# A set of seven half products in layer 1 of blocks 3 to 6, fixed staging tiles, C11 grown on M1, and a later check of the bounds

## The chip, the cores and the metric

The kernel runs on one core of a Trainium2 chip. The metric is the device time of one execution in microseconds (us). Times of engines come from one profiled execution.

## The reference, cut to what matters

B = 8 batches, H = 8 heads, S = 576 tokens, D = 64, 16 beacon keys ahead of the keys, DM = H * D = 512, rank 32, hidden width FF = 2048.

```
k_all  = concat(beacon_k, k);  v_all = concat(beacon_v, v)
scores = q @ k_all^T / sqrt(D);  masked causally over the S keys, beacons open
x      = softmax(scores) @ v_all            # per head, then heads side by side: (B, S, 512)
h      = (x^T @ U) @ V                      # mixes the 576 tokens of a batch, rank 32
u      = x + h^T
out    = u + max(u @ w_ch1, 0) @ w_ch2      # 512 -> 2048 -> 512
```

## The kernel before

**Tiling.** The attention goes by batch and pair of heads, the mixer by batch, and the two layers of the perceptron by blocks of 512 tokens, nine blocks (0 to 8) over all 8 x 576 tokens. All matrix work is in float16 with float32 sums. The transposed u (`uT`) lies in SBUF as a ring, channels on partitions; `uT` is made by transposing DMAs from x (`xb`) and by adding the mixer's products on VectorE (L476).

**One stream of work.** Every block of the perceptron is cut into small units of work, which go into one queue (`queue`). The attention code for the next batches calls `fill(n)` (L1180) between its own steps, and each call takes n units from the queue; so TensorE's instructions alternate between attention and perceptron. `fill` also issues one waiting step of the list `coming` (loads, weights made by GpSimd) per unit, and stores that have become due. Every engine runs its instructions in the order in which they were issued. `long_slot` (L1383) is the hand-written order for the later batches, `visit` (L395) does scores and exps in it, `mix` (L1250 and on) puts the mixer's steps into the queue, the loop at L1435 to L1466 goes over the pairs of heads.

**PSUM.** Eight banks go round in the order of their freeing: `pst` (L108) takes one, `emptying` (L115) gives it back.

**Layer 1.** Block 0 is computed plainly (`mlp_units`, L922). For blocks 1 to 8 `fast_units` (L595) makes the units. In blocks 1 to 6 layer 1 is sixteen `g_unit`s (L628 to L647): each is one tile of 128 hidden channels by 512 tokens, four matmuls (eight where the block wraps round the ring, as in block 4), whose relu is done by VectorE in units 2, 5, 11 and 13 and by ScalarE in the others. In blocks 7 and 8 (`QUADS`, L1163) layer 1 is done by `g_quads` (L649): three sets of four channel tiles each are computed as a 2 x 2 block product by seven half products in place of eight, in the manner of Strassen and Winograd. `step(q, n)` (L700 and on) is one step of set q: step 0 forms a product in bank A, which ScalarE copies to `lk`, and one in bank F, to which VectorE adds the copy; step 1 lets A grow by a second product (copied again) and begins D; step 2 lets A grow a third time (copied again), and VectorE adds the copy to D; step 3 ends A (relu by ScalarE) and D (sum and relu by VectorE). One half product is four matmuls of 256 columns (L674). The sums of weights that this needs (`lw`) are made by GpSimd (`quad_weights`, L580, four operations a set, L588), those of u by VectorE (L655, four a block), at the start of the block. A copy of bank A must be done before TensorE lets A grow again.

**Layer 2.** It is a 2 x 2 block product by seven products M1 to M7 in blocks 1 to 8; its sums of the hidden layer, called s1 to s4 in `sums` (L624), are made by VectorE while layer 1 still goes on (`SUMS`, L1164). In blocks 1 to 6 the units are `c_unit`s (L833), two a product, 14 in all; after each product `after(k)` (L795) adds: product 0 (bank A, M1) is copied by ScalarE, product 1 (bank F) is added to the copy by VectorE and gives C11, and C22, C21 and C12 follow. `residual` (GpSimd, L780) then adds u to each of the four quarters, from the tile `ut`, to which SP's queue transposes `uT` back (L611, issued in every second unit of layer 1); the quarter is then stored. In blocks 7 and 8 `chain_units` (L842) lets some products grow on one another's banks.

**Staging.** The q and k of a batch are loaded to two tiles of a pool `stage` with two buffers (`qk_tiles`, L253). Shortly before block 7, `quad_tiles` (L569) takes tiles from the same pool for the sums of weights, for those of u and for the copies of bank A.

**The check of the bounds.** `guard` (L997) is nine VectorE operations, which test the reciprocals of the softmax's sums; it is called once, right after the last mixer step has been put into the queue, and so falls into layer 1 of block 6. `guard_sum` (L1009) adds the result over partitions on TensorE; it stands in block 7. The answer decides at a branch near the end whether the slow exact path runs.

## Time and profile before

| | |
|---|---|
| time, median of 3 runs | 335.64 us (335.51 to 335.74) |
| the profiled execution | 336.39 us |
| its span | 334.5 us |
| TensorE busy | 326.3 us, 98% |
| VectorE, ScalarE, GpSimd busy | 251.7, 190.8, 148.5 us |
| layer 1 of blocks 3, 4, 5, 6, 7, 8 begins at | 146.00, 180.58, 215.32, 249.90, 279.1, 304.3 us |

The span is the time from the first to the last instruction in the profile; the execution's own time is 1.9 us longer. In the lines, PE is TensorE's matmuls, PEld its loads of weights, DVE VectorE, ACT ScalarE, POOL GpSimd, SP SyncE, which issues most DMAs (SPq is its queue). A line of the timeline gives the start, the time from there to the end of the last of the xN instructions, the engine, the line of the program, the operation, out<-in with shape and type, and in brackets how long the engine had been idle and what released it. A line of a group gives the busy time and the mean ns of one operation behind the bar.

### The profile page before, as it was taken

Reading aid. Unit: us, or ns where it says so; the run is one execution under the profiler, and the core shown is the slowest. Engines: PE = TensorE matmul, PEld = TensorE weight load, DVE = VectorE, ACT = ScalarE, POOL = GpSimd, SP = SyncE. Lnnn points to the kernel's source line nnn. Section 1 sums busy time; section 2 is a strip of 40 time slices with the busy share of each in tenths; the row PEclk is TensorE's granted clock in tenths of the full one; section 3 lists DMA queues with packets and bytes.
Section 4 is the critical chain, followed back from the end, with each engine's and each line's share of the span. In section 5 each row is a group of like instructions: output and inputs, shape, how many; then the busy total and the mean of one; then the engine's idle time right before and its main releaser. Section 6 shows DMA issues by size and latency. Waiting matters only on the chain.

```text
span 334.5 us, 9085 instructions
## 1 busy us (share of the span) xinstructions
PE 326.3 (98%) x3614; PEld 223.9 (67%) x3614; DVE 251.7 (75%) x572; ACT 190.8 (57%) x413; POOL 148.5 (44%) x185
## 2 busy tenths in 40 slices
PE   8899999999999999999999999999999999999993
PEld 3565555555577656865588888754875588788793
DVE  6675888678897668765777677667777978797692
ACT  5967961788972677257734684469435403703700
POOL 8987824766236540677066904150398014010010
PEclk9999999999999999999999999999999999999999
DMA  8999999999999993999999996955213513206113
GB/s 164 144 176 161 158 201 196 199 184 151 81 150 150 135 181 74 130 200 171 151 124 174 144 132 110 117 130 120 51 42 94 91 47 110 49 32 127 31 36 101
DMA packets 150561, 41.99 MB, mean 126 GB/s; under 512 B 131312, under 2 KB 149936, under 8 KB 150512
## 3 DMA queue, kind: packets, MB, share of 16 engines
q0 software_dynamic: 87568, 18.18, 73.3%
q1 hardware_dynamic: 62144, 22.41, 36.5%
q10 hardware_dynamic: 800, 0.75, 0.7%
q8 instruction: 30, 0.49, 0.6%
q14 instruction: 19, 0.16, 0.2%
HBM read 37.45 MB, written 9.44 MB: 140 GB/s over the span
## 4 chain that ended last, share of the span: by engine, by line
PE 91%; ACT 5%; DVE 1%; issue 0%
PE gps L635 24%; PE po L427 8%; PE mpsD L760 6%; PE sps L409 6%; PE mpsF L760 4%; PE cps L965 4%; PE mpsA L854 4%; PE gps L939 4%; PE mpsE L760 3%; PE qpsA L674 3%; PE mpsC L760 3%; PE mpsA L760 3%; PE mpsB L760 3%; ACT expt L376 2%; PE mpsD L854 2%; PE gps L663 2%
## 5 line engine op out<-in xcount | busy, mean ns | idle before, releaser
L418 ACT ACTIVATE expt<-sps 128x496 f16<-128x496 f32 (+2 forms) x192 | 82.2, 547 | 41.6 <-PE sps L409 41.6
L635 PE MATMUL gps<-uT,w 128*128 128x512 f16 (+1 forms) x448 | 91.9, 349 | 0.2 <-ACT kT L1091 0.2
L780 POOL TENSOR_TENSOR ob<-ob,ut 128x512 f32<-128x512 f32 x26 | 31.3, 1207 | 131.2 <-DVE ob L780 121.5
L760 PEld LDWEIGHTS <-gT 128*128 128x128 f16 x704 | 66.4, 98 | 10.4 <-issue 2.6
L635 PEld LDWEIGHTS <-w 128*128 128x128 f16 x448 | 40.4, 98 | 32.0 <-issue 2.5
L646 ACT ACTIVATE gT<-gps 128x512 f16<-128x512 f32 x72 | 42.9, 619 | 25.2 <-PE gps L635 19.9
L624 DVE TENSOR_TENSOR gT<-gT 128x1024 f16<-128x1024 f16 (+3 forms) x90 | 47.5, 550 | 1.0
L240 POOL DMA_DIRECT2D vs<-in_v_dram x50 | 39.9, 812 | 14.1 <-DMA w<-in_moe_w_ch_dram 11.1
L427 PEld LDWEIGHTS <-expt 128*128 128x128 f16 x900 | 33.8, 98 | 9.8 <-issue 1.5
L427 PE MATMUL po<-vs,expt 128*128 128x65 f16 x900 | 36.4, 194 | 0.3
L348 DVE TENSOR_TENSOR expt<-expt,bigmask 128x768 f16<-128x768 f16 x54 | 34.4, 676 | 1.4 <-ACT expt L418 1.2
L436 DVE TENSOR_TENSOR xb<-po,rec 128x320 f16<-128x320 f32 x64 | 31.5, 492 | 2.2
L435 DVE RECIPROCAL rec<-po 128x5 f32<-128x5 f32 x64 | 12.1, 189 | 19.5 <-PE po L427 19.1
L644 DVE TENSOR_SCALAR gT<-gps 128x512 f16<-128x512 f32 x24 | 16.6, 690 | 13.1 <-PE gps L635 12.6
L686 ACT ACTIVATE lk<-qpsA 128x512 f32<-128x512 f32 x18 | 10.3, 597 | 25.6 <-PE qpsA L674 14.8
L409 PE MATMUL sps<-qT,kT 64*128 64x80 f16 (+4 forms) x288 | 22.6, 281 | 0.0
L376 ACT ACTIVATE expt<-sps 128x496 f16<-128x496 f32 (+2 forms) x48 | 20.4, 569 | 0.7 <-PE sps L370 0.7
L854 PEld LDWEIGHTS <-gT 128*128 128x128 f16 x208 | 19.0, 98 | 2.4
L1038 POOL DMA_DIRECT2D st<-in_q_dram x20 | 16.9, 866 | 6.9 <-DVE ob L780 6.5
L409 PEld LDWEIGHTS <-kT 64*128 64x128 f16 x288 | 10.3, 94 | 12.8 <-issue 8.2
L1038 POOL DMA_DIRECT2D st<-in_k_dram x20 | 16.9, 859 | 1.5 <-DMA st<-in_q_dram 1.5
L939 PE MATMUL gps<-uT,w 128*128 128x512 f16 x64 | 16.2, 380 | 0.1
(151 smaller groups left out, 479.3 us busy)
## 6 DMA issues: line engine op xcount, KB each, us to landing
out_dram<-ob SPq DMA_DIRECT2D x33, 256.0 KB, 3.6
vs<-in_v_dram POOLq DMA_DIRECT2D x18, 128.0 KB, 6.9
w<-in_moe_w_ch_dram POOLq DMA_DIRECT2D x4, 512.0 KB, 6.4
w<-in_moe_w_ch_dram POOLq DMA_DIRECT2D x2, 1024.0 KB, 12.8
st<-in_k_dram POOLq DMA_DIRECT2D x12, 128.0 KB, 6.3
st<-in_q_dram POOLq DMA_DIRECT2D x12, 128.0 KB, 7.0
st<-in_k_dram POOLq DMA_DIRECT2D x4, 288.0 KB, 11.8
st<-in_q_dram POOLq DMA_DIRECT2D x4, 288.0 KB, 12.9
```

The lines of the kernel that those rows point to most:

```text
L240: nc.gpsimd.dma_start(out=dst[a : a + nq[j], j, :, :], in_=src[hs, ds(q0[j], nq[j]), :].rearrange("h p d -> p h d"))
L348: nc.vector.tensor_tensor(out=e, in0=e, in1=bigmask[:, :, :].rearrange("p (a b) x -> p a b x", b=2), op=ALU.min)
L409: nc.tensor.matmul(banks[i][:, ds(at0 + o, w)], kT(hp, c, ch), qT[hp, c, ds(qa, w)], start=True, stop=True, skip_group_check=len(unit) > 1,)
L418: nc.scalar.activation(out=at[p][3][i][:, ds(AT[g], gw[g])], in_=bank[:, ds(at0, gw[g])], func=AF.Exp, scale=scale)
L427: nc.tensor.matmul(po[:, j, :], ex[0 : nk[c], ds(blk[(c, j)], P)], vs[0 : nk[c], ds(c * H * E + h * E, E)], start=(c == 0), stop=(c == j),)
L436: nc.vector.tensor_tensor(out=xb[:, :, ds(h * D, D)], in0=po[:, :, 0:D], in1=r.broadcast_to([P, NT, D]), op=ALU.mult)
L624: nc.vector.tensor_tensor(out=o[:, ds(d0, n)], in0=x[:, ds(d0, n)], in1=y[:, ds(d0, n)], op=op)
L635: nc.tensor.matmul(g[:, ds(o, w)], w1[:, cc, ts(dc, P)], uT[:, cc, ds(at, w)], start=(cc == 0 and o == 0), stop=(cc == NCC - 1), skip_grou ...
L646: nc.scalar.activation(out=cell["g"][:, dc, :], in_=g, func=AF.Relu)
L760: nc.tensor.matmul(ps, a()[:, d, ds(P * i, P)], bm[:, d, ds(c0, w)], start=fresh and d == 0 and i == 0, stop=d == HF - 1, skip_group_check ...
L854: nc.tensor.matmul(ps, a()[:, d, ds(P * i, P)], bm[:, d, ds(c0, w)], start=fresh and d == 0, stop=d == HF - 1, skip_group_check=True,)
L1038: coming.append(lambda d=dst, s=src, a=m[j] - nq[j], n=m[j], j=j: nc.gpsimd.dma_start(out=d[a:n, j, :, :], in_=s[:, ds(q0[j], nq[j]), :].r ...
```

## The change

1. **One set in blocks 3 to 6.** `PARTS` takes the place of `QUADS`: blocks 3 to 6 do one set of four channel tiles (0, 1, 8, 9) by seven half products, the twelve other tiles as before; blocks 7 and 8 do three sets as before. The sixteen units are ordered tile 2, step 0, tile 10, step 1, tile 3, step 2, tile 11, tile 4, step 3, tiles 12, 5, 13, 6, 14, 7, 15. The plain tiles at places 2, 11 and 13 have their relu by VectorE. The sums s1 to s4 move to later units.
2. **Sums of u ahead.** For these four blocks the four subtractions of u are issued in the c-units 10 to 13 of the block before (`AHEAD`), by VectorE for blocks 3 and 4 and by GpSimd for blocks 5 and 6.
3. **C11 grown on M1.** In blocks 3 to 6 product 1 grows on product 0's banks, half by half; ScalarE copies the halves of M1 and later those of C11. Bank F and VectorE's add of C11 go.
4. **Fixed staging tiles.** Four constant tiles `staged` take the place of the pool `stage`; a batch uses the pair of its parity. The sums of u and of the weights of sets 1 and 2, and the copies of bank A for these sets, lie in parts of them; set 0's weights lie in tiles of the pool `pairs` and are made once, at an earlier pair of heads than before.
5. **The check later.** `guard` is put into the queue behind C11 of block 7, ahead of the unit whose result VectorE adds next; `guard_sum` stands three units later than before.

```diff
+    staged = [const.tile([P, TJ * DM], F16, name=f"st{i}", tag=f"st{i}") for i in range(4)]
-    def qk_tiles():
-        t = [stage.tile([P, TJ * DM], F16, name=f"st{i}", tag=f"st{i}") for i in range(2)]
+    def qk_tiles(b=0):
+        t = staged[2 * (b % 2) : 2 * (b % 2) + 2]
...
+    def quad_tiles(q):
+        if q == 0:
+            w = [pairs.tile([P, 512], F16, name=f"lw{k}", tag=f"pr{k % 2}") for k in range(4)]
+        else:
+            w = [staged[q - 1][:, ds(512 * k, 512)] for k in range(4)]
+            f = staged[q + 1][:, 0 : 2048].bitcast(F32).rearrange("p (k i x) -> p k i x", k=2, i=2)
+            lq["k", q] = (f[:, 0], f[:, 1], f[:, 0])
+        lq["w", q] = [x.rearrange("p (c f) -> p c f", c=2) for x in w]
+    def u_sums(t0, eng):
+        b11, b12, b21, b22 = (u_half(t0, c, x) for c in (0, 2) for x in (0, HT))
+        t1, t2, t3, t4 = (staged[i][:, 5 * DM : 6 * DM].rearrange("p (c x) -> p c x", c=2) for i in range(4))
+        lq["t"] = [t1, t2, t3, t4]
+        def one(o, x, y):
+            eng.tensor_tensor(out=o, in0=x, in1=y, op=ALU.subtract)
+        return [lambda a=a: one(*a) for a in ((t1, b12, b11), (t2, b22, t1), (t3, b22, b12), (t4, b21, t2))]
...
+            if not quads:
+                slots = [2, (0, 0), 10, (0, 1), 3, (0, 2), 11, 4, (0, 3), 12, 5, 13, 6, 14, 7, 15]
+                late = {11: ((0, 0, 4),), 12: ((1, 0, 4),), 13: ((2, 0, 4),), 14: ((0, 4, 3),), 15: ((1, 4, 3),)}
...
+        if parts:
+            sums_at = {0: ((2, 4, 3),), 1: ((0, 7, 1), (1, 7, 1)), 2: ((2, 7, 1), (3, 0, 4)), 3: ((3, 4, 4),)}
...
+        def second_on(i, c0, w):
+            ps = grown(1, "A", i, c0, w)
+            if i == 0:
+                out_tile("11")
+            nc.scalar.activation(out=obs["11"][:, i, :], in_=ps, func=AF.Copy)
+            freed(("A", i, c0))
+            if i:
+                residual("11", 0, 0)
         def c_unit(k, j):
-            bank = products[k][0]
-            p = pieces(bank)[j]
-            product(*products[k], *p)
+            p = pieces(products[k][0])[j]
+            if parts and k < 2:
+                (first, second_on)[k](*p)
+            else:
+                product(*products[k], *p)
...
+            for u in ahead(2 * k + j) if ahead else ():
+                u()
-            if j == 1:
+            if j == 1 and not (parts and k < 2):
                 after(k)
...
-    QUADS = (7, 8)
+    PARTS = {3: 1, 4: 1, 5: 1, 6: 1, 7: 3, 8: 3}
+    AHEAD = 10
...
+                us.extend(u_sums(512 * t, nc.vector if t < 5 else nc.gpsimd))
...
+            if p == P6 + 3:
+                quad_tiles(0)
+                coming.extend(quad_weights(0))
             if p == NP - 3:
-                quad_tiles()
-                coming.extend([u for q in range(3) for u in quad_weights(q)])
+                for n in (1, 2):
+                    quad_tiles(n)
+                    coming.extend(quad_weights(n))
...
         mix(B - 1)
-        guard()
-        queue.insert(len(queue) - 37, guard_sum)
+        queue.insert(len(queue) - 41, guard)
+        queue.insert(len(queue) - 34, guard_sum)
```

More of the change, by code (lines that the diff above doesn't have):

```diff
@@ L92 @@
     const = ctx.enter_context(tc.tile_pool(name="const", bufs=1))
-    stage = ctx.enter_context(tc.tile_pool(name="stage", bufs=2))
     pairs = ctx.enter_context(tc.tile_pool(name="pairs", bufs=2))
@@ L506, in end @@
             settle(1, uT[:, :, ds(u0 % RING + QM, n)], ups)
+            settled.add(u0 // S)
             emptying(ups)
@@ L565, in halves_of_w2, with u_half @@
         ]
-    lq = {}
-    def quad_tiles():
-        t = [stage.tile([P, TJ * DM], F16, name=f"lw{i}", tag=f"st{i}") for i in range(2)]
-        w = [[x[:, ds(512 * k, 512)] for k in range(4)] for x in t]
-        w.append([pairs.tile([P, 512], F16, name=f"lw{k}", tag=f"pr{k % 2}") for k in range(4)])
-        lq["w"] = [[x.rearrange("p (c f) -> p c f", c=2) for x in y] for y in w]
-        lq["t"] = [x[:, ds(4 * 512 + 512 * k, 512)].rearrange("p (c x) -> p c x", c=2) for x in t for k in range(2)]
-        f = [stage.tile([P, 3, 512], F32, name=f"lk{i}", tag=f"st{i}") for i in range(2)]
-        k = [x[:, i, :].rearrange("p (i x) -> p i x", i=2) for x in f for i in range(3)]
-        lq["k"] = [(k[2 * q], k[2 * q + 1], k[2 * q]) for q in range(3)]
+    lq, settled = {}, set()
+    def quad_tiles(q):
[6 more added lines that the diff above has]
+        lq["w", q] = [x.rearrange("p (c f) -> p c f", c=2) for x in w]
+    def u_half(t0, c0, x):
+        return uT[:, ds(c0, 2), ds((t0 + x) % RING, HT)]
+    def u_sums(t0, eng):
[3 more added lines that the diff above has]
+        def one(o, x, y):
+            assert (t0 + 511) // S in settled
+            eng.tensor_tensor(out=o, in0=x, in1=y, op=ALU.subtract)
+        return [lambda a=a: one(*a) for a in ((t1, b12, b11), (t2, b22, t1), (t3, b22, b12), (t4, b21, t2))]
     def quad_weights(q):
@@ L585, in quad_weights @@
         a11, a12, a21, a22 = part(0, 2 * q), part(2, 2 * q), part(0, HF + 2 * q), part(2, HF + 2 * q)
-        s1, s2, s3, s4 = lq["w"][q]
+        s1, s2, s3, s4 = lq["w", q]
         return [
@@ L593, in quad_weights, with fast_units @@
         ]
-    def fast_units(t0, dst, last=False, quads=False):
+    def fast_units(t0, dst, last=False, parts=0, ahead=None):
         cell, banks, obs = {}, {}, {}
+        quads = parts > 1
         cols = u_cols(t0, 512)
@@ L630, in g_unit, with between, layer_one @@
                 begin()
-            dc = order[k]
+            def between():
+                if k % 2 and cell["turns"]:
+                    cell["turns"].pop(0)()
+                for x in SUMS.get(k, ()):
+                    sums(*x)
+            layer_one(order[k], k in (2, 5, 11, 13), between)
+        def layer_one(dc, on_vector, between=lambda: None):
             g = pst([P, 512], F32, name="gps")
@@ L638, in g_unit @@
                     )
-            if k % 2 and cell["turns"]:
-                cell["turns"].pop(0)()
-            for x in SUMS.get(k, ()):
-                sums(*x)
-            if k in (2, 5, 11, 13):
+            between()
+            if on_vector:
                 nc.vector.tensor_scalar_max(out=cell["g"][:, dc, :], in0=g, scalar1=0.0)
@@ L649, in g_quads, with plain @@
         def g_quads():
-            at = t0 % RING
-            b11, b12, b21, b22 = (uT[:, ds(c, 2), ds(at + x, HT)] for c in (0, 2) for x in (0, HT))
+            b11, b12, b21, b22 = (u_half(t0, c, x) for c in (0, 2) for x in (0, HT))
+            us = u_sums(t0, nc.vector)
             t1, t2, t3, t4 = lq["t"]
-            us = [
-                lambda o=o, x=x, y=y: nc.vector.tensor_tensor(out=o, in0=x, in1=y, op=ALU.subtract)
-                for o, x, y in ((t1, b12, b11), (t2, b22, t1), (t3, b22, b12), (t4, b21, t2))
-            ]
             held = {}
-            def plain(dc):
-                g = pst([P, 512], F32, name="gps")
-                for cc in range(NCC):
-                    nc.tensor.matmul(
-                        g, w1[:, cc, ts(dc, P)], uT[:, cc, ds(at, 512)], start=cc == 0, stop=cc == NCC - 1
-                    )
-                nc.scalar.activation(out=cell["g"][:, dc, :], in_=g, func=AF.Relu)
-                emptying(g)
+            def plain(k, dc):
+                layer_one(dc, not quads and k in (2, 11, 13))
             def half(q, bank, a, b, fresh):
@@ L682, in of_lw, with space @@
             def of_lw(q, k):
-                return lambda c, i: lq["w"][q][k][:, c, ts(i, P)]
+                return lambda c, i: lq["w", q][k][:, c, ts(i, P)]
+            def space(q, k):
+                if k < 2:
+                    cell["k", q, k] = lq["k", q][k] if q else kept("k")
+                else:
+                    cell["k", q, k] = cell["k", q, 0]
+                return cell["k", q, k]
             def copied(q, k):
-                nc.scalar.activation(out=lq["k"][q][k], in_=held[q, "A"], func=AF.Copy)
+                nc.scalar.activation(out=space(q, k), in_=held[q, "A"], func=AF.Copy)
             def summed(q, bank, k, d, x):
                 nc.vector.tensor_tensor(
-                    out=cell["g"][:, ds(d, 2), ds(x, HT)], in0=held[q, bank], in1=lq["k"][q][k], op=ALU.add
+                    out=cell["g"][:, ds(d, 2), ds(x, HT)], in0=held[q, bank], in1=cell["k", q, k], op=ALU.add
                 )
@@ L720, in step, with unit @@
                     relu(cell["g"][:, :, HT:512].rearrange("p (h d) t -> p h d t", h=2)[:, :, ds(d, 2), :])
+            if not quads:
+                slots = [2, (0, 0), 10, (0, 1), 3, (0, 2), 11, 4, (0, 3), 12, 5, 13, 6, 14, 7, 15]
+                late = {11: ((0, 0, 4),), 12: ((1, 0, 4),), 13: ((2, 0, 4),), 14: ((0, 4, 3),), 15: ((1, 4, 3),)}
+                def unit(k, slot):
+                    if k == 0:
+                        begin()
+                    plain(k, slot) if isinstance(slot, int) else step(*slot)
+                    if k % 2 and cell["turns"]:
+                        cell["turns"].pop(0)()
+                    for x in late.get(k, ()):
+                        sums(*x)
+                return [lambda k=k, slot=slot: unit(k, slot) for k, slot in enumerate(slots)]
             slots = [
@@ L734, in unit @@
                 if isinstance(slot, int):
-                    plain(slot)
+                    plain(k, slot)
                 else:
@@ L831, in fast_units, with grown, first @@
         ]
-        def c_unit(k, j):
-            bank = products[k][0]
-            p = pieces(bank)[j]
-            product(*products[k], *p)
+        def grown(k, name, i, c0, w):
+            _, a, bm, _ = products[k]
+            fresh = (name, i, c0) not in banks
+            if fresh:
+                banks[name, i, c0] = pst([P, w], F32, name="mps" + name)
+            ps = banks[name, i, c0]
+            for d in range(HF):
+                nc.tensor.matmul(
+                    ps, a()[:, d, ds(P * i, P)], bm[:, d, ds(c0, w)],
+                    start=fresh and d == 0, stop=d == HF - 1, skip_group_check=True,
+                )
+            return ps
+        def first(i, c0, w):
+            ps = grown(0, "A", i, c0, w)
+            if i == 0:
+                kept("s1")
+            nc.scalar.activation(out=cell["s1"][:, i, :], in_=ps, func=AF.Copy)
+        def second_on(i, c0, w):
+            ps = grown(1, "A", i, c0, w)
+            if i == 0:
+                out_tile("11")
[3 more added lines that the diff above has]
+                residual("11", 0, 0)
+        def c_unit(k, j):
+            p = pieces(products[k][0])[j]
+            if parts and k < 2:
+                (first, second_on)[k](*p)
+            else:
+                product(*products[k], *p)
             for x in sums_at.get(2 * k + j, ()):
                 sums(*x)
-            if j == 1:
+            for u in ahead(2 * k + j) if ahead else ():
+                u()
+            if j == 1 and not (parts and k < 2):
                 after(k)
@@ L845, in chain_units @@
             small = [(0, 0, HC), (1, 0, P), (1, P, P)] if last else halves
-            def grown(k, name, i, c0, w):
-                _, a, bm, _ = products[k]
-                fresh = (name, i, c0) not in banks
-                if fresh:
-                    banks[name, i, c0] = pst([P, w], F32, name="mps" + name)
-                ps = banks[name, i, c0]
-                for d in range(HF):
-                    nc.tensor.matmul(
-                        ps, a()[:, d, ds(P * i, P)], bm[:, d, ds(c0, w)],
-                        start=fresh and d == 0, stop=d == HF - 1, skip_group_check=True,
-                    )
-                return ps
-            def first(i, c0, w):
-                ps = grown(0, "A", i, c0, w)
-                if i == 0:
-                    kept("s1")
-                nc.scalar.activation(out=cell["s1"][:, i, :], in_=ps, func=AF.Copy)
             def second(i, c0, w):
@@ L917, in fast_units @@
             return g_quads() + chain_units()
-        units = [lambda k=k: g_unit(k) for k in range(NDC)]
+        units = g_quads() if parts else [lambda k=k: g_unit(k) for k in range(NDC)]
         units += [lambda k=k, j=j: c_unit(k, j) for k in range(7) for j in range(len(pieces(products[k][0])))]
@@ L1023, in load_batch @@
         if b < DT0:
-            Ls[b] = qk_tiles()
+            Ls[b] = qk_tiles(b)
             emit_loads(b, Ls[b], vss[b % 2])
@@ L1030, in load_whole @@
     def load_whole(b):
-        Ls[b] = qk_tiles()
+        Ls[b] = qk_tiles(b)
         for i, (src, m) in enumerate(((k[b], nk), (q[b], nq))):
@@ L1191, in fill, with sums_ahead, at @@
             n -= 1
+    def sums_ahead(t):
+        if PARTS.get(t, 0) != 1:
+            return None
+        us = []
+        def at(n):
+            if n == AHEAD:
+                us.extend(u_sums(512 * t, nc.vector if t < 5 else nc.gpsimd))
+            return us[n - AHEAD : n - AHEAD + 1] if n >= AHEAD else []
+        return at
     def feed(b):
@@ L1203, in feed @@
             else:
-                units = fast_units(512 * t, dst, t == NBLK - 1, t in QUADS)
+                units = fast_units(512 * t, dst, t == NBLK - 1, PARTS.get(t, 0), sums_ahead(t + 1))
             queue.extend(units)
@@ L1272 @@
         emit_w1(0)
-        Ls[1] = qk_tiles()
+        Ls[1] = qk_tiles(1)
         (kt, qt), _ = Ls[1]
```

## The prediction

> **What bounds the kernel now.** I read the head of the profile's page first, then its chain of work that ended last, then busy time by stage (cut where TensorE starts a block's layer 1), then timelines of single engines around each edit.

> ```profile
> span 334.5 us, 9085 instructions
> ...
> PE 326.3 (98%) x3614; PEld 223.9 (67%) x3614; DVE 251.7 (75%) x572; ACT 190.8 (57%) x413; POOL 148.5 (44%) x185
> ...
> PE 91%; ACT 5%; DVE 1%; issue 0%
> ```

> TensorE is busy 98% of the span and is 91% of the chain that ended last. So a matmul saved shortens the kernel by its duration, and a pause of TensorE lengthens it by the pause.

> The stages (columns: stretch, its length, then busy time and instructions of PE, PEld, DVE, ACT, POOL; granted clock; DMA share; GB/s):

> ```profile
> 146.00:180.58 34.58, 34.58 (x374) 22.83 (x373) 24.78 (x52) 20.76 (x45) 18.44 (x22) 1.00 1.76 162
> 180.58:215.32 34.74, 34.74 (x437) 28.97 (x436) 24.77 (x52) 20.77 (x45) 16.42 (x20) 1.00 1.50 134
> 215.32:249.90 34.58, 34.58 (x373) 22.78 (x372) 24.99 (x51) 20.76 (x45) 14.82 (x13) 1.00 0.46 82
> 249.90:279.10 29.20, 29.20 (x270) 19.42 (x269) 23.43 (x47) 8.74 (x15) 11.16 (x10) 1.00 0.33 75
> ```

> These four rows are blocks 3 to 6, the ones whose layer 1 changes. TensorE pauses in none of them. VectorE, ScalarE and GpSimd have 6 to 20 us idle in each, so the sum of their added work fits; what matters is whether single results come in time.

> **The change part by part.**

> *1. Fewer products (blocks 3 to 6).* Rows of the chain, the last a run of 256-column matmuls:

> ```profile
> 146.00 0.86 PE gps L635 x4
> ...
> 150.03 4.42 PE gps L635 x20
> ...
> 219.35 4.42 PE gps L635 x20
> ...
> 284.63 1.31 PE qpsA L674 x12
> ```

> A 512-column matmul takes 0.865 / 4 = 0.216 us (a plain unit of four; 4.42 / 20 = 0.221 has what stands between units in it), one of 256 columns 1.31 / 12 = 0.109. Per block 16 x 0.216 = 3.46 become 28 x 0.109 = 3.06: -0.40, four times -1.6.

> *2. ScalarE's copies, blocks 3 and 4.* The growing bank A is copied by ScalarE after its first, second and third state, and TensorE's next matmuls into it wait for the copy. After unit 2 ScalarE has four exps to do, and by the order of instructions they stand ahead of the second copy. Block 3 now:

> ```profile
> 149.86 2.01 ACT L418 ACTIVATE expt<-sps 128x496 f16<-128x496 f32 x4 [1.05 <-PE sps L409]
> 151.73 1.12 ACT L646 ACTIVATE gT<-gps 128x512 f16<-128x512 f32 x2
> ...
> 279.75 0.60 ACT L686 ACTIVATE lk<-qpsA 128x512 f32<-128x512 f32 x1 [11.39 <-PE qpsA L674]
> ```

> and for the step from one engine to TensorE, block 7 (VectorE's sums, then the two TensorE products that need them):

> ```profile
> 279.99 0.41 DVE L655 TENSOR_TENSOR lw<-uT 128x512 f16<-128x512 f16 x1
> 280.44 1.26 DVE L655 TENSOR_TENSOR lw<-uT,lw 128x512 f16<-128x512 f16 x1
> ...
> 281.85 0.60 PE L674 MATMUL qpsA<-lw 128*128 128x256 f16 x4
> 282.28 0.60 PE L674 MATMUL qpsD<-lw 128*128 128x256 f16 x4
> ```

> 281.85 - (280.44 + 1.26) = 0.15 us. Unit 3 starts at 150.03 and is (0,1), eight small matmuls, 0.87; unit 4 is a plain tile, 0.87; unit 5 is the third half product into A, due at 151.77. ScalarE is free at 151.73, copies 0.60, and the signal takes 0.15: 152.48. A pause of 0.7. Block 4 has the same order: +1.4 for both; between nothing (if the copy got ahead of the exps) and 1.6. In block 5 the wait of step 3 covers it, in block 6 only two exps stand there, half of 2.01, and the copy is in time.

> *3. Block 5: sums of u on GpSimd.* The four subtractions of u are taken ahead, in the c-units 10 to 13 of the block before: by VectorE for blocks 3 and 4, by GpSimd for 5 and 6. GpSimd's order of instructions around block 4's end becomes: residual C22, s1, s2, residual C21, s3, s4, residual C12. Residual C22 adds u back, which comes by the transposes ut. The trace of before:

> ```profile
> 191.19 0.49 DVE L436 TENSOR_TENSOR xb<-po,rec 128x320 f16<-128x320 f32 x1
> ...
> 191.71 7.25 SPq L455 DMA_TRANSPOSE uT<-xb x5
> ...
> 213.15 2.52 SPq L611 DMA_TRANSPOSE ut<-uT  x2
> ...
> 220.17 3.74 POOL L780 TENSOR_TENSOR ob<-ob,ut 128x512 f32<-128x512 f32 x3 [9.55 <-DMA ut<-uT]
> ```

> GpSimd waits 9.55 us for the last two ut transposes and adds C22 only at 220.17, already inside block 5 (from 215.32). Nobody on TensorE needs these residuals, so that costs nothing today. After the change s1 and s2 are queued behind that wait, and unit 3 of block 5, (0,1), multiplies with s2. SP's queue is occupied back to back from 191.71 to 215.67 (five uT, two ut, one kT, five qT, one kT, two ut), and it starts with VectorE's last xb. In block 4 that xb now has a sum of D or F and its relu ahead of it:

> ```profile
> L689 DVE TENSOR_TENSOR gT<-qpsD,lk 128x512 f16<-128x512 f32 x12 | 7.9, 685 | 4.1 <-ACT lk L686 2.2 <-PE qpsD L674 1.9
> ...
> L694 DVE TENSOR_SCALAR gT<-gT 128x1024 f16<-128x1024 f16 x6 | 2.6, 427 | 0.2
> ```

> 1.1 us, of which I take 0.75, with the 0.3 that block 3 is late by: ut lands at 221.2. GpSimd's adds of this size take 1.16 and follow each other at 1.11 (rows in step 4): 221.2 + 1.11 + 1.11 + 1.16 = 224.6, seen by TensorE at 224.75. Unit 3 would be due at 219.35, +0.56 for blocks 3 and 4 (2 x 0.7 - 2 x 0.40, less a rounding): 219.91. Pause 4.84. Then unit 5 needs s3, behind residual C21: 224.6 + 1.11 + 1.11 + 0.15 = 226.95, against 224.75 + 1.74 = 226.49: another 0.46. Together **+5.3**. Least 4.5 (xb no later); most 6.2 (three adds slowed to the 1.47 of the row in step 4).

> *4. Block 6, the same on GpSimd.*

> ```profile
> 239.86 1.16 POOL L780 TENSOR_TENSOR ob<-ob,ut 128x512 f32<-128x512 f32 x1 [14.83 <-DVE ob L780]
> 240.97 1.16 POOL L588 TENSOR_TENSOR lw<-lw,w 128x512 f16<-128x512 f16 x1
> ...
> 250.39 1.47 POOL L588 TENSOR_TENSOR lw<-w 128x512 f16<-128x512 f16 x1
> ...
> 236.84 2.91 ACT L418 ACTIVATE expt<-sps 128x496 f16<-128x496 f32 x6
> ...
> 292.92 0.38 ACT L864 ACTIVATE kept<-mpsA 128x256 f32<-128x256 f32 x1 [0.28 <-PE mpsA L854]
> ...
> 253.72 4.42 PE gps L635 x20
> ```

> C11 grows on M1's bank now and is copied out by ScalarE in two halves behind six exps (239.75 + 2 x 0.38 = 240.5), where VectorE added it; residual C11 starts 0.7 later, 240.56. It and ten more operations through s2 at 1.11: 252.8, or 253.5 with two slowed to 1.5. Unit 3 is due at 253.72: no pause. s3 comes two operations on, 255.75, +0.15; unit 5 is due at 253.72 + 1.74 = 255.46. **+0.4** (0 to 0.9).

> *5. The bounds' check behind C11 of block 7.*

> ```profile
> 261.30 0.33 DVE L999 MEMSET good<- 128x320 f16 x1
> ...
> 263.94 0.68 DVE L624 TENSOR_TENSOR gT<-gT 128x1024 f16<-128x1024 f16 x1
> ...
> 296.06 0.69 DVE L780 TENSOR_TENSOR ob<-mpsF,kept 128x512 f32<-128x512 f32 x1
> 296.67 0.41 DVE L780 TENSOR_TENSOR ob<-mpsA,ut 128x256 f32<-128x256 f32 x1
> 297.00 1.53 DVE L624 TENSOR_TENSOR gT<-gT 128x1024 f16<-128x1024 f16 x1
> 298.45 0.41 DVE L780 TENSOR_TENSOR ob<-mpsA,ut 128x256 f32<-128x256 f32 x1
> ...
> 300.16 0.42 DVE L780 TENSOR_TENSOR ob<-mpsA,ut 128x256 f32<-128x256 f32 x1
> ...
> 299.02 3.67 PE L854 MATMUL mpsA<-wt,gT 128*128 128x256 f16 x32
> ...
> 296.83 1.15 POOL L780 TENSOR_TENSOR ob<-ob,ut 128x512 f32<-128x512 f32 x1 [15.41 <-DVE ob L780]
> ```

> The nine operations take 263.94 - 261.30 = 2.64. They are taken from block 6, where VectorE is not waited for, and put between 296.06's add and 296.67's. The add of A then ends at 296.67 + 2.64 + 0.41 = 299.72, with the signal 299.87, and TensorE's third product into that bank, due at 299.02, waits 0.9 (rounded up). The other half's add (0.34 from start to start) and three sums (0.60 each, as 263.94's row goes on) follow, and the next add ends at 302.2; the fourth product, due at 299.87 + 2 x 0.87 = 301.6, waits 0.7: **+1.6**. Least 0.9 (the second wait absorbed), most 2.5: GpSimd's residual of 296.83 runs just there, and beside it the sum at 297.00 took 1.53 where the one at 263.94 took 0.68.
> [...]

> *6. At nothing:* the fixed staging tiles (two pairs by parity of the batch, as the pool of two gave; if a load had to wait, GpSimd's 16 idle us in block 3's row cover it); set 0's weights made earlier (4 of 1.16 us in that idle time); bank F saved; relus moved between VectorE and ScalarE, both idle ten us a block.

> Sum: -1.6 + 1.4 + 5.3 + 0.4 + 1.6 = +7.1. The profiled execution took 336.39, 1.9 of it around the span, and would take 343.5; the median of the runs is 335.64, so they would take **342.7**.

> **The rivals.**

> *A, as summed.* 342.7; its terms' ends give 339.4 to 345.2.

> *B, the pause in block 5 slows the clock.* At the start of the span:

> ```profile
> 1.19 3.60 PE idle L273 x8
> ```

> 0.45 for a 512-column matmul against 0.216: TensorE starts at half rate. If 4.8 us of pause bring that back, the first eight cost 8 x 0.234 = +1.9: 344.6. Against: the granted clock is 1.00 in every stretch above, but no stretch holds a pause of that length.
> [...]

> *C, the check stays hidden*, because VectorE has caught up by 296 or the product has a bank to spare: 342.7 - 1.6 = 341.1. Against: VectorE is back to back from 296.06 to 298.8.

> *D, GpSimd is not held.* If the transposes land by 216 (5 us earlier), s2 is there before 219.9; 342.7 - 5.3 = 337.4. Against: SP's order is the same, and its queue has no gap to give.

> *E, not slower: TensorE passes over a matmul that waits* and does later ones into other banks. Then the pauses of steps 2 to 5 are filled by other units, and only -1.6 is left: 334.0. It decides from the point at which a free matmul stands behind the held one. Against: the product into D needs only the sum that ended at 279.99 + 0.41 = 280.40, while the one into A needs the sum of 281.70; D stood behind A and began at 282.28, after it.

> **How the numbers follow.** A 0.50, B 0.26, C 0.09, D 0.09, E 0.06. The time is A's, 342.7. A's low end less the check's least 0.9 is 338.5, where C may lie; B's upper end is 345.2 + 1.9, about 347: 338.5 to 347.0, which leaves out D, E and a little of the tails. 0.2% of 335.64 is 0.67 us, about what a measurement of this kernel can tell from no change. Faster is E, less a case in which a small term stays: 0.05; within 0.2% 0.02; slower 0.93.

> **What would show it.** Block 3's layer 1 is 0.3 us longer, with (0,2) beginning right after the second copy. In block 5, GpSimd's row of C22 near 221, s1 and s2 behind it, and TensorE idle about 5 us ahead of (0,1), released by GpSimd: this carries the forecast. Matmuls at 0.43 behind that pause would show B. In block 7 the product into A waits for VectorE about 1 us behind the check's nine rows. The forecast is wrong if GpSimd's sums come ahead of C22 in time, or if block 5's window stays under 35 us.

## The result and the profile after

The changed kernel takes 344.86 us (median; 343.43 to 345.74), the kernel before 335.62 us (335.51 to 335.9): ratio 1.0268, 95% interval 1.0246 to 1.029. It is slower by 9.2 us, inside the range; the forecast case gave 342.7, the rival with the slowed clock 344.6.

The head of the page of the changed kernel, and its chain that ended last by engine:

```profile
span 343.2 us, 9193 instructions
...
PE 327.6 (95%) x3646; PEld 227.4 (66%) x3646; DVE 260.9 (76%) x592; ACT 196.7 (57%) x429; POOL 158.5 (46%) x193
...
PE 74%; POOL 7%; DVE 5%; DMA 4%; ACT 4%; issue 3%; SPq 1%; POOLq 0%; DVEq 0%
```

TensorE's share of the chain falls from 91% to 74%, and GpSimd is on it now. Busy time by stage, cut again where a block's layer 1 begins (PE, PEld, DVE, ACT, POOL; clock; DMA):

```profile
146.03:180.91 34.88, 34.34 (x386) 24.00 (x385) 27.79 (x59) 22.12 (x49) 18.55 (x22) 1.00 1.85 149
180.91:215.89 34.98, 34.45 (x433) 28.56 (x432) 26.21 (x57) 22.12 (x49) 16.41 (x20) 1.00 1.58 138
215.89:256.95 41.06, 37.15 (x386) 25.10 (x384) 26.14 (x54) 22.34 (x49) 19.08 (x17) 0.92 0.36 71
256.95:286.04 29.09, 28.99 (x283) 20.61 (x281) 22.65 (x41) 10.26 (x19) 11.54 (x10) 1.00 0.30 76
286.04:313.74 27.70, 25.58 (x216) 20.57 (x214) 23.88 (x52) 10.00 (x18) 2.87 (x3) 1.00 0.27 70
313.74:343.20 29.46, 25.05 (x230) 20.96 (x227) 20.96 (x45) 10.00 (x18) 1.15 (x1) 0.99 0.26 73
```

Against the stages of before: block 3 +0.30, block 4 +0.24, block 5 +6.48, block 6 -0.11, block 7 +2.50 (25.20 before), the last block -0.74 (30.20 before; TensorE's part of it is the same, the stores at the end were done sooner), and 0.03 ahead of block 3. The sum is 8.7, the difference of the spans. The profiled execution of before (336.39) was 0.75 above the median of its kernel, that of after 0.08, and later runs of the kernel before with 335.5 to 335.7 us have spans of 333.6 to 333.9; so the -0.74 probably belongs to that one execution and not to the change. Block 5 and block 7 carry the loss, and block 5's granted clock is 0.92.

From here on s1 to s4 are the four sums of u, as in the prediction, and unit 3 of a block is step 1 of its set, (0,1). Block 5, timeline of GpSimd, then of TensorE:

```profile
219.81 1.15 POOL L820 TENSOR_TENSOR ob<-ob,ut 128x512 f32<-128x512 f32 x1 [8.21 <-DMA ut<-uT]
220.92 1.46 POOL L593 TENSOR_TENSOR st<-uT 128x512 f16<-128x512 f16 x1
222.46 1.34 POOL L593 TENSOR_TENSOR st<-uT,st 128x512 f16<-128x512 f16 x1
```

```profile
223.85 1.01 PE L690 MATMUL qpsA<-st,lw 128*128 128x256 f16 x4 [3.91 <-POOL st L593]
224.66 1.06 PE L690 MATMUL qpsD<-st,lw 128*128 128x256 f16 x4
225.51 1.91 PE L664 MATMUL gps<-uT,w 128*128 128x512 f16 x4
227.22 1.06 PE L690 MATMUL qpsA<-st,lw 128*128 128x256 f16 x4
...
231.12 0.60 PE L690 MATMUL qpsA<-st,w 128*128 128x256 f16 x4
```

s1 and s2 stand behind residual C22, which waits for the transposes; TensorE pauses 3.9 us and then runs at half rate: four plain matmuls from 225.51 to 227.22 take 1.71 in place of 0.865, four of 256 columns are shown as 1.01 in place of 0.60. The rate is back after the fourth unit behind the pause, at about 229.8. The granted clock of the changed kernel in stretches of 3.4 us:

```profile
222.90:226.30 3.40, 2.45 (x10) 1.47 (x10) 0.00 (x0) 0.60 (x1) 3.40 (x4) 0.51 0.13 44
226.30:229.70 3.40, 3.40 (x11) 1.52 (x10) 0.69 (x1) 1.19 (x2) 3.05 (x3) 0.50 0.42 122
229.70:233.10 3.40, 3.40 (x55) 2.53 (x53) 1.55 (x4) 1.91 (x4) 0.00 (x0) 0.98 0.64 144
```

It is 0.5 from about 222.9 to 229.7. Of that TensorE worked from 223.85, 5.85 us at half rate: 2.9 us lost. With the pause (unit 3 due at 219.9, begun at 223.85) that is 6.9, less 0.40 of saved matmuls: the 6.48.

Block 7, VectorE, GpSimd and TensorE:

```profile
303.60 0.33 DVE L1053 MEMSET good<- 128x320 f16 x1
303.96 0.98 DVE L1056 TENSOR_SCALAR good<-rec 112x64 f16<-112x64 f32 x1
...
307.10 0.42 DVE L820 TENSOR_TENSOR ob<-mpsA,ut 128x256 f32<-128x256 f32 x1
```

```profile
303.67 1.16 POOL L820 TENSOR_TENSOR ob<-ob,ut 128x512 f32<-128x512 f32 x1 [15.32 <-DVE ob L820]
```

```profile
307.58 2.08 PE L880 MATMUL mpsA<-wt,gT 128*128 128x256 f16 x16 [1.73 <-DVE ob L820]
310.05 1.03 PE L880 MATMUL mpsA<-wt,gT 128*128 128x256 f16 x8 [0.38 <-DVE ob L820]
```

The check takes 307.10 - 303.60 = 3.50, not 2.64; its first comparison, 0.26 before, took 0.98, until GpSimd's residual was over (304.83). TensorE waits twice, at the two places that were named.

### The profile page after: what moved, and what is told of

Same layout as the page of the kernel before. It is cut to its first block, busy times and chain, and to the rows that moved or that the text cites. A ratio compares the mean times of both kernels' runs of the same rounds, so it can differ in the third digit from the quotient of the medians.

```text
span 343.2 us, 9193 instructions
## 1 busy us (share of the span) xinstructions
PE 327.6 (95%) x3646; PEld 227.4 (66%) x3646; DVE 260.9 (76%) x592; ACT 196.7 (57%) x429; POOL 158.5 (46%) x193
## 3 DMA queue, kind: packets, MB, share of 16 engines
q1 hardware_dynamic: 62144, 22.41, 34.9%
## 4 chain that ended last, share of the span: by engine, by line
PE 74%; POOL 7%; DVE 5%; DMA 4%; ACT 4%; issue 3%; SPq 1%; POOLq 0%; DVEq 0%
PE gps L664 20%; PE po L428 7%; PE mpsA L880 6%; PE sps L410 5%; PE qpsA L690 5%; PE cps L1019 4%; PE mpsD L800 4%; PE gps L993 4%; DMA vs<-in_v_dram 3%; ACT expt L419 3%; PE mpsE L800 2%; PE mpsC L800 2%; PE mpsB L800 2%; PE qpsD L690 2%; POOL st L605 2%
## 5 line engine op out<-in xcount | busy, mean ns | idle before, releaser
L419 ACT ACTIVATE expt<-sps 128x496 f16<-128x496 f32 (+2 forms) x192 | 82.2, 543 | 43.3 <-PE sps L410 43.3
L664 PE MATMUL gps<-uT,w 128*128 128x512 f16 (+1 forms) x400 | 86.6, 359 | 0.2 <-ACT kT L1145 0.2
L664 PEld LDWEIGHTS <-w 128*128 128x128 f16 x400 | 37.1, 99 | 30.1 <-issue 3.5
L672 ACT ACTIVATE gT<-gps 128x512 f16<-128x512 f32 x68 | 40.8, 616 | 23.4 <-PE gps L664 17.9
L642 DVE TENSOR_TENSOR gT<-gT 128x1024 f16<-128x1024 f16 (+3 forms) x90 | 46.5, 541 | 0.9
L349 DVE TENSOR_TENSOR expt<-expt,bigmask 128x768 f16<-128x768 f16 x54 | 36.0, 706 | 0.4 <-ACT expt L419 0.2
L709 ACT ACTIVATE kept<-qpsA 128x512 f32<-128x512 f32 x18 | 10.8, 601 | 29.2 <-PE qpsA L690 15.7
L436 DVE RECIPROCAL rec<-po 128x5 f32<-128x5 f32 x64 | 12.0, 188 | 17.1 <-PE po L428 16.8
L670 DVE TENSOR_SCALAR gT<-gps 128x512 f16<-128x512 f32 x20 | 13.8, 689 | 11.6 <-PE gps L664 11.4
L712 DVE TENSOR_TENSOR gT<-qpsD,kept 128x512 f16<-128x512 f32 x12 | 8.3, 691 | 14.4 <-ACT kept L709 11.8
L880 PE MATMUL mpsA<-w,gT 128*128 128x256 f16 x160 | 19.0, 273 | 0.0
L410 PEld LDWEIGHTS <-kT 64*128 64x128 f16 x288 | 10.2, 94 | 12.8 <-issue 8.2
```

The lines of the kernel that those rows point to most:

```text
L349: nc.vector.tensor_tensor(out=e, in0=e, in1=bigmask[:, :, :].rearrange("p (a b) x -> p a b x", b=2), op=ALU.min)
L410: nc.tensor.matmul(banks[i][:, ds(at0 + o, w)], kT(hp, c, ch), qT[hp, c, ds(qa, w)], start=True, stop=True, skip_group_check=len(unit) > 1,)
L419: nc.scalar.activation(out=at[p][3][i][:, ds(AT[g], gw[g])], in_=bank[:, ds(at0, gw[g])], func=AF.Exp, scale=scale)
L642: nc.vector.tensor_tensor(out=o[:, ds(d0, n)], in0=x[:, ds(d0, n)], in1=y[:, ds(d0, n)], op=op)
L664: nc.tensor.matmul(g[:, ds(o, w)], w1[:, cc, ts(dc, P)], uT[:, cc, ds(at, w)], start=(cc == 0 and o == 0), stop=(cc == NCC - 1), skip_grou ...
L672: nc.scalar.activation(out=cell["g"][:, dc, :], in_=g, func=AF.Relu)
```

## The experiments

Each is the changed kernel with the edit shown; times are medians.

**1. Block 5's sums of u on VectorE.**

```diff
-                us.extend(u_sums(512 * t, nc.vector if t < 5 else nc.gpsimd))
+                us.extend(u_sums(512 * t, nc.gpsimd if t == 6 else nc.vector))
```

> The changed kernel with block 5's four sums of u on VectorE, as for blocks 3 and 4. Theory (GpSimd's s1 and s2 behind residual C22, 3.9 us of pause, and then matmuls at half rate, 2.9 us): both go together, block 5's stage falls from 41.06 us to 34.9 (34.58 less 0.40, plus the wait for the copy of 0.7 that appears as in blocks 3 and 4), the granted clock of the stage is 1.00 and the time about 338.7. First rival (the half rate has another cause, such as more matmuls of 256 columns in a row): the pause goes, the slow matmuls stay, about 341.5. Second rival (VectorE has no room for four more sums and becomes late): 340 or more with TensorE waiting for VectorE in block 5.

338.57 us, 0.8% above the kernel before (ratio 1.0083, 1.0066 to 1.01). Its stage of block 5:

```profile
216.08:250.96 34.88, 34.34 (x386) 23.94 (x384) 26.39 (x56) 22.12 (x49) 14.62 (x13) 1.00 0.50 84
```

Pause and slow matmuls went together, and the wait for the copy appeared in block 5 as a third one: 0.54 of idle time, 0.70 by the length of the stage (34.88, and 34.18 where experiment 8 has removed it). The two rivals fall.

**2. The check where it was.**

```diff
-        queue.insert(len(queue) - 41, guard)
+        guard()
```

> The changed kernel with the bounds' check issued where it was before, in block 6, all else as changed. Theory (the nine operations stand between C11's add and the next bank's add, 2.1 us of waits, 2.5 us more in block 7's stage): block 7's stage falls from 27.70 us to 25.2 and block 6's does not grow; the time falls by 2.5. Rival (block 7's stage is longer because of something else in the change, the staging tiles or the sums of u on the same engine): it stays above 26.5.

341.77 us, 3.1 below the changed kernel. Block 7, and the clock behind block 5's pause, which is as long as before (3.95 idle, 3.91 in the changed kernel):

```profile
284.21:309.30 25.09, 25.09 (x216) 20.67 (x214) 21.50 (x43) 10.00 (x18) 2.73 (x3) 1.00 0.31 74
```

```profile
222.80:226.00 3.20, 2.48 (x10) 1.43 (x10) 0.00 (x0) 0.60 (x1) 3.20 (x4) 0.50 0.15 51
226.20:229.20 3.00, 3.00 (x31) 1.79 (x29) 0.69 (x1) 2.00 (x4) 2.83 (x3) 1.00 0.34 94
```

Block 7 gains 2.6, as the theory has it; block 6 takes 29.25, 0.16 more. The execution shown is the shortest of the four, 340.41, and in it the slow stretch was 3.4 us long and not 6.8. Its mean clock is 0.995; two more runs have that too, and the fourth (342.69) has 0.987. So the rest of the gain seems to be that more of these runs had the short stretch, not an effect of the edit; of the runs that were not profiled only the mean clock is on record.

**3. and 4. A shorter and a longer pause.** In the first, the four sums of u of block 5 are issued one unit earlier, so that s1 stands ahead of residual C22; in the second s1 is issued three times (both cut to the main lines):

```diff
+            at0 = AHEAD - 1 if t == 5 else AHEAD
-            return us[n - AHEAD : n - AHEAD + 1] if n >= AHEAD else []
+            return us[n - at0 : n - at0 + 1] if n >= at0 else []
```

```diff
+            mine = us[n - AHEAD : n - AHEAD + 1] if n >= AHEAD else []
+            return mine * 3 if t == 5 and n == AHEAD else mine
```

> The changed kernel with block 5's sums of u on GpSimd one unit earlier: s1 comes ahead of residual C22, only s2 behind it. Theory of the clock (a pause must last some 3 us or more before the rate halves): the pause ahead of step 1 falls by one addition, to about 2.5 us, no matmul behind it is slow, and block 5's stage is about 36.9 us against 41.06. Rival (any pause of TensorE costs a slow stretch): the stage is about 39.7, with matmuls of 256 columns at 0.21 behind the pause.

342.42 us, but the four runs lie between 340.91 and 345.71. The one that was profiled is the longest, and in it the transposes came late: C22 began at 222.38, 5.4 us into the block and not 3.9, and the pause was 3.57.

```profile
224.73 1.01 PE L690 MATMUL qpsA<-st,lw 128*128 128x256 f16 x4 [3.57 <-POOL st L593]
```

The clock was 0.5 from 223.2 to 230.0 in it. So this profile doesn't show a short pause. The two shortest runs, 341.03 and 340.91, have a mean clock of 0.997, too high for a slow stretch (one of 3.4 us at half rate in 340 us makes it 0.995), and lie near the theory's 340.7 (344.86 less 41.06 - 36.9). It seems that a shorter pause passed without half rate there, but its length in those runs isn't on record; experiment 6 asks again. No run had shown the theory's 3 us: past the start of the span, the waits measured until then were one of 3.91 us with the half rate behind it and others of up to 1.73 us without.

> The changed kernel with block 5's s1 computed three times over on GpSimd, so that s2 comes two additions later; nothing is left out of the result. Theory of the clock: the pause grows by 2.2 to 2.9 us, to 6.1 to 6.8, and the slow stretch behind it costs again about 2.9 us, since it ends after a time of activity and not after a number that grows with the pause: block 5's stage is 43.3 to 44. Rival (the slow stretch grows with the pause): 44.8 or more. The pause also tells whether residual C22's start, by the last transposes, or GpSimd's own work sets it: by the theory C22 starts at the same place in the stage as before the edit.

347.82 us. The pause was 6.98, more than forecast, since C22 was again late (5.3 us into the block, and not at the same place); the stage was 44.4, between the theory and the rival. The clock was low for 10.2 us:

```profile
222.40:225.80 3.40, 0.00 (x0) 0.00 (x0) 0.00 (x0) 0.00 (x0) 3.16 (x4) 0.50 0.23 77
225.80:229.20 3.40, 2.27 (x10) 1.43 (x10) 0.00 (x0) 0.60 (x1) 3.40 (x4) 0.50 0.08 28
229.20:232.50 3.30, 3.30 (x12) 1.40 (x10) 0.48 (x1) 1.19 (x2) 3.23 (x3) 0.50 0.41 115
232.60:235.60 3.00, 3.00 (x46) 2.24 (x45) 1.26 (x4) 1.79 (x3) 0.00 (x0) 1.00 0.94 139
```

The longer pause adds idle time at low clock, but TensorE worked at half rate from 226.93 to 232.5, 5.6 us, no longer than with 3.9 us of pause: the theory's 2.8.

**5. The check ahead of C11's add** (`len(queue) - 43` in place of `- 41`).

> The changed kernel with the bounds' check issued before C11's add of block 7 and not behind it, so that GpSimd's residual C11 (303.67 us in the changed kernel) cannot run beside its first operations. Theory (one of the check's operations on float32 reciprocals was held by that residual: 0.98 us where its like took 0.26): the nine operations take 2.64 us and not 3.50, the held one is back at 0.26, and the residual now runs beside the adds or the sum behind C11, which then are the ones held (a sum of 0.68 becomes about 1.5). Rival (that operation is slow for another reason, such as its first read of the reciprocals): it is 0.98 again.

345.49 us in a single execution, with C22 late again and a pause of 4.68 in block 5, so the time says nothing of this edit. Its VectorE and GpSimd in block 7:

```profile
303.85 0.26 DVE L1056 TENSOR_SCALAR good<-rec 112x64 f16<-112x64 f32 x1
...
306.24 0.69 DVE L820 TENSOR_TENSOR ob<-mpsF,kept 128x512 f32<-128x512 f32 x1
...
307.18 1.53 DVE L642 TENSOR_TENSOR gT<-gT 128x1024 f16<-128x1024 f16 x1
```

```profile
307.01 1.15 POOL L820 TENSOR_TENSOR ob<-ob,ut 128x512 f32<-128x512 f32 x1 [18.18 <-DVE ob L820]
```

The nine operations take 2.75 in place of 3.50, the comparison is back at 0.26, and the sum beside the residual takes 1.53 in place of 0.68. So the residual held the comparison in one order and the sum in the other. TensorE's two waits there fall only from 1.73 + 0.38 to 0.97 + 0.86.

**6. and 7. Pauses of other lengths at another place.** Both have experiment 1's edit; the check's reduction is issued three or seven times:

```diff
+        for _ in range(3):
-        nc.vector.tensor_reduce(out=allg, in_=good, op=ALU.min, axis=AX.XY)
+            nc.vector.tensor_reduce(out=allg, in_=good, op=ALU.min, axis=AX.XY)
```

> The kernel with block 5's sums of u on VectorE, whose only long pause is that of block 7 behind the check (1.60 us), and the check's reduction issued three times in place of once (nothing is left out; two more of about 0.5 us). Theory (the rate halves only behind a pause that fills most of some 3 us): a pause of 2.6 us in block 7, and behind it matmuls of 256 columns at 0.109 as always; time 338.57 + 1.0 = 339.6, with a spread below 0.6 us over the runs. Rival (any pause of 2 us or more halves it): matmuls at 0.21 behind the pause for 2.5 us or more, 341 or more.

340.31 us. TensorE's pause, and the clock behind it:

```profile
302.28 4.49 PE L880 MATMUL mpsA<-wt,gT 128*128 128x256 f16 x24 [2.63 <-DVE ob L820]
```

```profile
302.20:303.20 1.00, 0.92 (x7) 0.59 (x7) 1.00 (x4) 0.00 (x0) 0.00 (x0) 1.00 0.00 0
303.50:306.70 3.20, 3.20 (x17) 2.00 (x15) 2.42 (x6) 0.00 (x0) 0.00 (x0) 0.50 0.02 5
307.00:310.20 3.20, 3.20 (x31) 2.87 (x30) 1.72 (x6) 0.05 (x1) 0.00 (x0) 1.00 0.52 165
```

My theory of the length fell: in this execution 2.63 us were enough. The rate halves only some 1.2 us after TensorE has begun again, and for one stretch of 3.4 us. The time lies between the theory's 339.6 and the rival's 341: TensorE, slowed, no longer waits a second time. And it isn't so in every run: one of the four, 340.01, has a mean clock of 1.000, which leaves no room for a slow stretch.

> The same with the reduction issued seven times (six more of about 0.5 us). Theory: a pause of 4.6 us in block 7, which halves the rate there just as the pause of 3.9 us on GpSimd did in block 5: matmuls at 0.21 behind it for 2.5 to 5.5 us; time 338.57 + 3.0 + 1.2 to 2.9 = 342.8 to 344.5, with a spread over the runs of 1 us or more. Rival (the half rate in block 5 belonged to that place, not to the pause): 341.6 with no slow matmul.

343.76 us. TensorE's pause:

```profile
304.37 5.28 PE L880 MATMUL mpsA<-wt,gT 128*128 128x256 f16 x24 [4.73 <-DVE ob L820]
```

The clock was 0.5 from 303.0 to 309.7: the half rate belongs to the pause and not to block 5 or to GpSimd. Three of the four runs lie within 0.12 us; the expected spread comes from one alone (346.75, with a mean clock of 0.977 against 0.988).

**8. to 11. Repairs.** Experiments 1 and 2 together, and step 2 of the set one tile later; then variants with block 6's sums on VectorE too, and with C11 made as before.

```diff
-                slots = [2, (0, 0), 10, (0, 1), 3, (0, 2), 11, 4, (0, 3), 12, 5, 13, 6, 14, 7, 15]
+                slots = [2, (0, 0), 10, (0, 1), 3, 11, (0, 2), 4, (0, 3), 12, 5, 13, 6, 14, 7, 15]
```

> The changed kernel with three repairs: the check issued where it was before, the sums of u of block 5 on VectorE, and step 2 of the set moved one plain tile later, so that ScalarE's second copy is done by then. Block 6's sums stay on GpSimd. Theory (the change's matmuls save 0.40 us a block, and its losses are the three waits): stages of blocks 3, 4, 5 at 34.2, 34.4, 34.2 us, block 7 at 25.1, time 334.1, 0.4% below the kernel before. Rival (moving the step only moves the wait, to step 3 or to VectorE's sum of D): stages of blocks 3 to 5 stay near 34.8, 335.7.

333.77 us: ratio to the kernel before 0.9934 (0.9921 to 0.9947). Stages of blocks 3 to 7:

```profile
146.14:180.32 34.18, 34.18 (x387) 23.98 (x385) 27.72 (x59) 21.94 (x49) 18.54 (x22) 1.00 1.89 151
180.32:214.62 34.30, 34.30 (x434) 28.62 (x432) 26.93 (x60) 21.96 (x49) 16.43 (x20) 1.00 1.63 142
214.62:248.80 34.18, 34.18 (x386) 23.93 (x384) 26.33 (x56) 21.94 (x49) 14.60 (x13) 1.00 0.51 85
248.80:277.78 28.98, 28.98 (x285) 20.76 (x283) 25.16 (x50) 10.14 (x19) 12.24 (x10) 1.00 0.30 76
277.78:302.87 25.09, 25.09 (x216) 20.65 (x214) 21.49 (x43) 10.00 (x18) 2.72 (x3) 1.00 0.28 79
```

TensorE is busy all the time again, and blocks 3, 4 and 5 are 0.40, 0.44 and 0.40 shorter than before the change.

> As the kernel with three repairs, and with block 6's sums of u on VectorE too. Theory: block 6's stage loses what is left of its wait, at most 0.3 us: 333.9 to 334.1. Rival (VectorE, 23 us of 29 busy in that stage, is late with the masks or the sums): block 6's stage is 29.3 or more.

333.89 us, ratio 0.9956 (0.9937 to 0.9974). Block 6's stage is 29.44, 0.46 longer than with GpSimd, as the rival has it; TensorE waits 0.17 there for an add of VectorE. But with C11 made as before (the next two runs) it is the other way round, 29.06 on VectorE and 29.48 on GpSimd, so these traces don't say which engine is better for block 6's sums.

> As the kernel before in this list, but C11 is made as before the change: product 1 in bank F, added by VectorE to the copy of M1, in blocks 3 to 6. Theory (C11 grown on M1 saves no matmul, and VectorE has 6 us or more idle a block): within 0.3 us of the kernel with all sums on VectorE. Rival (it frees VectorE or a bank that the set needs): 0.5 us or more slower, with TensorE waiting for VectorE.

333.58 us, ratio 0.9936 (0.9923 to 0.9948).

> The kernel with three repairs, block 6's sums of u on GpSimd, and C11 made as before the change. Theory (C11's edit is worth nothing beyond what VectorE has idle): 333.6 to 333.8, the same as with C11 grown on M1. Rival (with block 6's sums on GpSimd an earlier residual C11 matters): up to 0.3 below that.

333.88 us, ratio 0.9948 (0.9927 to 0.997). The four versions can't be told apart; C11 grown on M1 is worth nothing that these runs show. All four beat both kernels, by 0.4 to 0.7% against the kernel before.

## Why the prediction was right, and where it was off

*Step 1, right.* -0.40, -0.44 and -0.40 in blocks 3 to 5, to be seen bare in the stages of experiment 8; block 6 is only 0.22 shorter there, which no run explains.

*Step 2, right.* TensorE's third product into A began at 152.46 in the changed kernel (forecast 152.48), behind the second copy, in block 4 likewise; one tile in between removes the wait.

```profile
152.46 0.60 PE L690 MATMUL qpsA<-st,lw 128*128 128x256 f16 x4 [0.54 <-ACT kept L709]
```

*Step 3, right in its mechanism, off in two sizes that partly cancel.* SP's queue did start later by about what was forecast (192.88 for 191.71), but the last transposes of `uT` started only 0.57 later (213.72 for 213.15):

```profile
192.88 7.19 SPq L456 DMA_TRANSPOSE uT<-xb  x5
...
213.72 3.12 SPq L629 DMA_TRANSPOSE ut<-uT  x2
```

C22 began at 219.81 and not at 221.2, and the pause ahead of unit 3 was 3.95 and not 4.84. In the eight profiled executions of the changed kernel and of experiments 1 to 7 C22 began 3.9 to 5.4 us into block 5, so this term is uncertain by 1.5 us in any single run. The 0.46 for s3 didn't come: s3 was ready at 226.02, and at half rate TensorE came to unit 5 only at 227.22.

*The choice between A and B was the wrong one.* B came true, and dearer: 2.9 us and not 1.9, because I priced eight matmuls as at the start of the span (0.45 us each, with the granted clock given as 1.00 there), while the low clock lasted 6.8 us here and half of the time worked in it is lost. That the sum of A came within 2.2 us of the measured time is in part luck: the pause and s3 that were priced 1.4 too high hide half of this missing term.

*Step 4, right.* s3 came 0.3 us late (unit 5 at 262.74, due at 262.48); the stage is 0.11 shorter, forecast 0.0.

*Step 5, the mechanism right, the term mis-sized:* 2.5 and not 1.6. That is its upper bound, 1.6 and the 0.85 by which the two rows of the sum differ (1.53 and 0.68), but not for the reason given there, a held sum: in the changed kernel that sum, at 307.44, took 0.68. In the 1.6 I let the check run at its old 2.64; beside GpSimd's residual its first comparison took 0.98, and 0.26 without it (experiment 5), 0.7 more. Rival C was contradicted.

*Step 6, as far as the runs show right:* C11 brings nothing (experiments 10 and 11). No run takes back the staging or the earlier weights alone, but the stages add up without a cost for them. D and E are contradicted by the pause itself: TensorE did nothing for 3.91 us and came to the plain tile behind the held products only at 225.51.

Sum by measured sizes: -0.40 -0.44 -0.40 -0.40 + 2 x 0.7 + 3.95 + 2.9 + 0.3 + 2.5 = 9.4 in TensorE's end, less 0.7 by the shorter tail of stores: 8.7 between the two profiled executions. The -0.40 of block 6 is the forecast one; with the 0.3 it comes near the measured -0.11. The medians differ by 9.2.

## What to carry to other kernels

Work that TensorE waits for must not be queued behind work that nobody waits for: here two subtractions of 1.3 to 1.5 us behind a residual that waited for a transpose cost 6.9 us, though GpSimd was idle for half of the stage (busy 19.08 of 41.06 us). In experiment 3 the first of them, issued one unit earlier, ran at 212.65, 9.7 us ahead of that residual. Read from the order of instructions what stands ahead on that engine and when its last input lands. In these profiles pauses of TensorE of 2.63 to 6.98 us had a low clock behind them, by which another 1.3 us (experiment 2) to 2.9 us (the changed kernel) of its work were lost, so removing such a wait can be worth more than its length: experiment 1 took away a pause of 3.91 us and 6.3 us of time.

## What the runs showed of the hardware that was not expected

A low clock isn't only found where a pause was built in. In later measurements one of 17 runs of the kernel before took 338.69 us with a mean clock of 0.989, and single runs of the repaired kernels 337.36 (0.990) and 336.99 (0.995). These runs were not profiled, so what set it off there stays open.
